# Weight and activation residues, state scaling and the norm's g moved from VectorE to GpSimd and ScalarE in a linear-attention and two-MoE kernel

## The chip, the cores and the metric

The kernel runs on one core of one Trainium2 chip. Its time is the device time in microseconds (us) of one launch; a median of several runs is given. Engines are named TensorE (PE in the profile, its weight loads PEld), VectorE (DVE), ScalarE (ACT), GpSimd (POOL) and SyncE (SP, which issues the DMAs).

## What is computed

Gated linear attention over 4 batches, 8 heads, 768 steps and a head size of 48, then two feed-forward blocks on the 3072 x 384 result. Weights arrive as 8-byte floats, all else as float32.

```python
for t in range(S):                      # attention, per batch and head
    state = alpha[t][:, None] * state + outer(k[t], v[t])
    y[t] = q[t] @ state
x = y as 3072 x 384
xn = x / sqrt(mean(x * x) + 1e-6) * rms_g        # first block, d_ff 1536
x = (silu(xn @ w_gate) * (xn @ w_val)) @ w_out
h = max(x @ w1, x @ w2, x @ w3)                  # second block, d_ff 768
out = h @ w_out2
```

## The kernel before

The attention is cut into 24 tiles of 128 steps (one batch, all heads; batches inside, steps outside). For each tile, class `Tile_` holds a chain: the loads of alpha, k, q (`ld`) and v (`lv`); for the first six tiles transposes on TensorE (`pa`), for the others on VectorE (`bt`); scans and products on VectorE that give R, kT (`br`) and aT, qT (`b`), with the old state scaled into Sd; transposed k and the scores on TensorE (`pb`); the scores masked on VectorE (`c`, tiles named at); state update and y on TensorE (`pc`); the sum of squares on ScalarE (`ss`), its root on GpSimd (`rr`, L702 and L705); the state's copy or sum (`st`); the normed, g-scaled row xn (`d`, L719); its transpose (`pd`); and the split of that into a rounded part xh (`eh`, ScalarE) and the residue xl (`el`, VectorE, L736).

Matmuls of the feed-forward blocks run on such pairs, a high part and a residue, in three products: high by high, residue by high, high by residue. The weights pass through class `Weights` in chunks of 128 x 384, two at a time: `load` (SP), `join` (VectorE, three instructions a chunk, L58 to L60, that make float32 out of the 8-byte words), `high` (ScalarE), `rest` (VectorE, the residue, L380) and `check` (ScalarE, two instructions on the raw words, L389 and L392, whose sums are looked at once at the end, by `flag`). There are 36 chunks of the first block, three for each of 12 columns blocks f (gate, val, out), and 24 of the second.

The first block runs in 96 slots, 12 for each of 8 blocks of 384 rows (three tiles); the slots of the first two blocks alternate in halves, so that slots 0 to 5 need the first 18 chunks and slots 12 to 17 the others. A slot has three groups of nine products on TensorE: gate, val (both at L769) and second (L816), with silu, a product on VectorE (`mu`, L802), and the split of the hidden row into hh (ScalarE) and hl (VectorE, L810) between them. The second block's 48 slots have four such groups.

The order of all this on each engine comes from a planner, class `Order`: each part has an engine, a cost, a due time (in slots) and the parts it needs; the planner plays this through and writes the instructions in the order found. Engines then run their own lists in that order and wait on semaphores. While TensorE has nothing to do before the first val product, the planner puts in filler products that nobody reads (`fill`, L776). The lines that set due times here:

```python
HEAD = (11, 2, 0, 1)
at = due(i) - (HEAD[i // 2] if first and i < 8 else 1 if first else 1.5)
if n < TPB:
    at, step = -20 + 2 * n, 0.5
elif n < 2 * TPB:
    at, step = -10 + 0.5 * (n - TPB), 1
```

Of the kernel before, what the change touches and what calls it, by code (L numbers as in the profile page):

```python
# [281 lines left out]
def gla_moe_moe(ctx: ExitStack, tc: tile.TileContext, q, k, v, alpha, wg, wv, wo, g, w1, w2, w3, wo2, out):  # L282
# [37 lines left out]
    HEAD = (11, 2, 0, 1)  # L320

    class Weights:


        def __init__(self, tag, pool, bufs, chunks, where, due, needs):

            self.tag, self.pool, self.raws, self.tmps = tag, pool, {}, {}
# [3 lines left out]
            for i in range(n):  # L331
                at = due(i) - 10 - (HEAD[i // 2] if first and i < 8 else 1.5)
                before = needs(i) + self.prev("load", i, 1) + self.prev("check", i, bufs)
                if i >= bufs:
                    before.append((tag, "join", (i - bufs) // 2 * 2))
                plan.add((tag, "load", i), "SP", 1.1, at, before, partial(self.load, i, bufs), later=LAT)
            for i in range(0, n, 2):
                both = [j for j in (i, i + 1) if j < n]
                at = due(i) - (HEAD[i // 2] if first and i < 8 else 1 if first else 1.5)
                plan.add((tag, "join", i), "DVE", 1.3 * len(both), at,  # L340
                         [(tag, "load", j) for j in both] + self.prev("rest", i, 2) + self.prev("join", i, 2),
                         partial(self.join, both))
                plan.add((tag, "high", i), "ACT", 0.45 * len(both), at, [(tag, "join", i)] + self.needed(needs, both),
                         partial(self.high, both))
# [9 lines left out]
        def needed(self, needs, both):  # L354
            return []

# [6 lines left out]
        def join(self, both):  # L363
            steps = []
            for i in both:
                self.tmps[i] = self.pool().tile([P, CW], F32, name="cv_t", bufs=2)
# [64 lines left out]
    gb = ap1.tile([P, DM], F32, name="gb")  # L431
# [8 lines left out]
    ends = ap1.tile([W, NP, P], F32, name="ends")  # L440
# [8 lines left out]
    column = ap1.tile([P, P], F32, name="column")  # L449
    place = ap1.tile([P, 32], F32, name="place")  # L450
# [31 lines left out]

    NPE = 6

    class Tile_:


        def __init__(self, n):
# [4 lines left out]

            if n < TPB:
                at, step = -20 + 2 * n, 0.5
            elif n < 2 * TPB:
                at, step = -10 + 0.5 * (n - TPB), 1
            elif n < 3 * TPB:
                at, step = 12 + 3 * (n - 2 * TPB), 1
            else:  # L500
                at, step = 21 + 4 * (n - 3 * TPB), 0.7
# [557 lines left out]
```

## Time and profile before

| | us |
|---|---|
| median of 3 runs | 906.6 (905.54 to 907.75) |
| the profiled execution | 905.86 |
| its span | 903.7 |
| TensorE busy in it | 886.8 |
| VectorE busy | 530.5 |
| ScalarE busy | 350.4 |
| GpSimd busy | 22.5 |

The span is what the profile covers of the profiled execution. Busy time of TensorE counts matmuls from start to modelled end, so overlaps and fillers count as busy. Idle time is shown ahead of the instruction that ended it, with what released it. The granted clock is 1.00 at TensorE's full 2.4 GHz. Instructions of one engine overlap a little: 0.55 us long, a VectorE residue is followed by the next after 0.47.

### The profile page before, as it was taken

What the parts mean: (1) busy time and instruction counts of PE and PEld (TensorE: products, weight loads), DVE (VectorE), ACT (ScalarE), POOL (GpSimd) and SP (SyncE); (2) the same over time, 40 slices, a digit from 0 to 9 for tenths busy, and PEclk for the clock granted to TensorE, in tenths of its full rate; (3) what the DMA queues carried; (4) which work ended last, traced back from release to release, by engine and by line L of the source; (5) the groups of instructions that cost most, each with busy time, mean ns of one, the idle gap of its engine ahead of it and who ended that gap; (6) DMA issues with size and microseconds to landing.
All of it is one profiled execution on the core that took longest, in us unless ns stands there. A gap on an engine that the chain in (4) does not pass through costs nothing.

```text
span 903.7 us, 16408 instructions
## 1 busy us (share of the span) xinstructions
PE 886.8 (98%) x6527; PEld 864.9 (96%) x6527; DVE 530.5 (59%) x1063; ACT 350.4 (39%) x898; POOL 22.5 (2%) x66
## 2 busy tenths in 40 slices
PE   7999999999999999999999999999999999999997
PEld 6889999999999999999999999999999999999996
DVE  8999999987666666666663377483332323323221
ACT  4578775333333223233233277561221212212121
POOL 1000000000000000000000000000000000000000
PEclk9999999999999999999999999999999999999999
DMA  9845654343223223223201145140110100101000
GB/s 196 190 114 159 193 168 131 101 123 84 58 57 85 57 58 84 58 58 81 61 10 45 36 131 164 39 140 17 37 53 1 53 27 27 53 1 53 1 27 30
DMA packets 106243, 69.17 MB, mean 77 GB/s; under 512 B 49200, under 2 KB 103856, under 8 KB 106160
## 3 DMA queue, kind: packets, MB, share of 16 engines
q1 hardware_dynamic: 106160, 68.05, 28.2%
q8 instruction: 53, 0.87, 0.4%
q14 instruction: 30, 0.25, 0.1%
HBM read 57.41 MB, written 10.62 MB: 75 GB/s over the span
## 4 chain that ended last, share of the span: by engine, by line
PE 89%; DVE 4%; DMA 3%; SPq 2%; ACT 1%; issue 1%; DVEq 0%; ACTq 0%
PE bank L769 56%; PE bank L816 15%; PE bank L969 8%; PE bank L653 2%; PE bank L691 2%; PE bank L685 2%; DMA raw<-in_moe_w_val_dram 1%; PE bank L676 1%; DVE cv_t L59 1%; DVE cv_t L60 1%; SPq L551 1%; PE bank L776 1%; PE bank L725 1%; SPq L562 1%; PE bank L646 1%
## 5 line engine op out<-in xcount | busy, mean ns | idle before, releaser
L954 DVE TENSOR_TENSOR sg<-sg,bank 128x384 f32<-128x384 f32 x96 | 53.2, 554 | 173.0 <-PE bank L769 172.7
L802 DVE TENSOR_TENSOR sg<-sg,bank 128x384 f32<-128x384 f32 x96 | 52.8, 550 | 94.5 <-PE bank L769 93.1
L806 ACT ACTIVATE hh<-sg 128x384 fp32r<-128x384 f32 x96 | 50.0, 520 | 134.4 <-DVE sg L802 134.3
L769 PE MATMUL bank<-xh,wgh 128*128 128x384 f32 x288 | 100.7, 350 | 0.0
L816 PE MATMUL bank<-hh,woh 128*128 128x384 f32 x288 | 98.3, 341 | 0.0
L769 PE MATMUL bank<-xl,wgh 128*128 128x384 f32 x288 | 97.2, 337 | 1.2 <-DVE xl L736 1.2
L816 PE MATMUL bank<-hl,woh 128*128 128x384 f32 x288 | 96.9, 336 | 1.3 <-DVE hl L810 1.3
L769 PE MATMUL bank<-xh,wgl 128*128 128x384 f32 x288 | 97.3, 338 | 0.1
L769 PE MATMUL bank<-xh,wvh 128*128 128x384 f32 x288 | 97.0, 337 | 0.0
L769 PE MATMUL bank<-xh,wvl 128*128 128x384 f32 x288 | 96.5, 335 | 0.0
L816 PE MATMUL bank<-hh,wol 128*128 128x384 f32 x288 | 96.4, 335 | 0.0
L769 PE MATMUL bank<-xl,wvh 128*128 128x384 f32 x288 | 96.3, 334 | 0.0
L958 ACT ACTIVATE hh<-sg 128x384 fp32r<-128x384 f32 x48 | 25.2, 525 | 160.0 <-DVE sg L954 160.0
L810 DVE TENSOR_TENSOR hl<-sg,hh 128x384 fp32r<-128x384 f32 x96 | 53.3, 555 | 31.3 <-ACT hh L806 31.3
L799 ACT ACTIVATE sg<-bank 128x384 f32<-128x384 f32 x96 | 46.7, 487 | 52.3 <-PE bank L769 51.3
L816 PEld LDWEIGHTS bank<-hl,woh 128*128 128x128 f32 x288 | 54.3, 188 | 2.4 <-DVE hl L810 2.3
L816 PEld LDWEIGHTS bank<-hh,woh 128*128 128x128 f32 x288 | 54.2, 188 | 1.8
L769 PEld LDWEIGHTS bank<-xl,wgh 128*128 128x128 f32 x288 | 54.5, 189 | 1.5 <-DVE xl L736 1.5
L769 PEld LDWEIGHTS bank<-xh,wgh 128*128 128x128 f32 x288 | 54.4, 189 | 1.5
L769 PEld LDWEIGHTS bank<-xh,wgl 128*128 128x128 f32 x288 | 54.5, 189 | 0.5 <-DVE wgl L380 0.5
L769 PEld LDWEIGHTS bank<-xh,wvh 128*128 128x128 f32 x288 | 54.1, 188 | 0.5 <-DVE sg L802 0.3
L816 PEld LDWEIGHTS bank<-hh,wol 128*128 128x128 f32 x288 | 54.2, 188 | 0.0
(138 smaller groups left out, 2010.9 us busy)
## 6 DMA issues: line engine op xcount, KB each, us to landing
raw<-in_moe_w_out_dram SPq DMA_DIRECT2D x18, 384.0 KB, 3.7
raw<-in_moe_w_dram SPq DMA_DIRECT2D x18, 384.0 KB, 3.8
y_scr<-yo SPq DMA_DIRECT2D x30, 192.0 KB, 2.0
raw<-in_moe_w_gate_dram SPq DMA_DIRECT2D x12, 384.0 KB, 4.3
vt<-in_v_dram SPq DMA_DIRECT2D x24, 192.0 KB, 2.7
raw<-in_moe_w_val_dram SPq DMA_DIRECT2D x12, 384.0 KB, 4.4
xl<-y_scr SPq DMA_DIRECT2D x8, 576.0 KB, 4.5
out_dram<-yo SPq DMA_DIRECT2D x24, 192.0 KB, 2.0
```

The costliest lines, as they stand in the source:

```text
L653: nc.tensor.matmul(self.sc[i][:, pr, :], self.kT[lo:hi, pr, :], self.qT[lo:hi, pr, :], start=True, stop=True)
L685: nc.tensor.matmul(self.y[tk, 2 * pr:2 * pr + 2, :].rearrange("p a d -> p (a d)"), self.qT[:, pr, tk], Sds[self.s][:, pr, :], start=True, ...
L691: nc.tensor.matmul(self.y[tk, 2 * pr + i, :], at[i][:, pr, tk], vt[:, 2 * pr + i, :], start=not self.c, stop=True, skip_group_check=True,)
L769: nc.tensor.matmul(ps, w_[:, kt, col], m_[:, kt, :], start=i == 0, stop=i == 3 * KT - 1)
L799: nc.scalar.activation(hid[s], banks[3][:, :NB], AF.Silu)
L802: nc.vector.tensor_tensor(hid[s], hid[s], banks[4][:, :NB], ALU.mult)
L806: nc.scalar.activation(hi_[s], hid[s], AF.Copy)
L810: nc.vector.tensor_tensor(lo_[s], hid.pop(s), hi_[s].bitcast(F32), ALU.subtract)
L816: nc.tensor.matmul(banks[e][:, :NB], w_[:, f, es], m_, start=f == f0 and i == 0, stop=f == f1 - 1 and i == 2)
L954: nc.vector.tensor_tensor(hid2[z], hid2[z], banks[3 + j][:, :NB], ALU.max)
L958: nc.scalar.activation(hi2[z], hid2[z], AF.Copy)
L969: nc.tensor.matmul(banks[t][:, :DM], l_[:, tsl], r_[:, f, :], start=f == 0 and i == 0, stop=f == NF2 - 1 and i == 2)
```

## The change

- The residues of the weights (`rest`), of both blocks, and of xt (`el`) go from VectorE to GpSimd. As GpSimd reads no PSUM here, ScalarE makes a second copy xf of the transposed row for it.
- The scaling of the old state into Sd goes to GpSimd, as a part of its own (`sd`, `carry`).
- g is no longer multiplied into xn: xn is made on ScalarE from y and the root alone, and GpSimd multiplies g into the gate and val chunks between `join` and `high` (`gain`; the tile gt holds g by columns).
- The first tiles' state copies (four tiles) go from VectorE to ScalarE; the square sums of kT are taken before those of qT.
- The first block's weights are checked later: each chunk is loaded a second time, from slot 27 on, and checked then. The buffer of a raw chunk is free for the next load after `join`, not after `check`; the joined chunks have four buffers instead of two.
- Due times of the first 12 tiles, of the transposes and of the chunks are new tables; the planner's cost of a group of products is 1.565 instead of 1.47.
- Some tiles share memory: column and place lie in aT, ends is BF16, xn has two buffers.

```diff
-    HEAD = (11, 2, 0, 1)
+    CV = 2
+    RAW = 4
+    AGAIN = 27
+    AHEAD = (
+        18.8, -3.3, 6.7, 4.1, 3, -3.1, 15.8, 2.3, -0.6, -0.8, 7.2, 23.8, 1.3, 1, 1, 1, 1, 1,
+    )
...
-                before = needs(i) + self.prev("load", i, 1) + self.prev("check", i, bufs)
+                before = needs(i) + self.prev("load", i, 1) + ([] if again else self.prev("check", i, bufs))
...
+                scaled = [j for j in both if self.scaled(j)]
+                if scaled:
+                    plan.add((tag, "gain", i), "POOL", 1.15 * len(scaled), at + 2.1, [(tag, "join", i), "gt"],
+                             partial(self.gain, scaled))
...
-                plan.add((tag, "rest", i), "DVE", 0.47 * len(both), at + 0.2, [(tag, "high", i)],
+                plan.add((tag, "rest", i), "POOL", 1.15 * len(both), at + (-4 if first else 0.2), [(tag, "high", i)],
                          partial(self.low, both))
                 for j in both:
-                    plan.add((tag, "check", j), "ACT", 1.42, at + 2, [(tag, "load", j)],
-                             partial(self.check, j))
+                    if again:
+                        old = [(tag, "check", j - bufs)] if j >= bufs else [(tag, "join", n - 2)]
+                        plan.add((tag, "load again", j), "SP", 1.1, again(j) - 2,
+                                 old + [(tag, "load again", j - 1) if j else (tag, "load", n - 1)],
+                                 partial(self.load, j, bufs), later=LAT)
+                    plan.add((tag, "check", j), "ACT", 1.42, again(j) if again else at + 2,
+                             [(tag, "load again" if again else "load", j)], partial(self.check, j))
...
+        def scaled(self, i):
+            return self.tag == "w1" and i % 3 < 2
+
+        def gain(self, which):
+            for i in which:
+                t = self.tmps[i].rearrange("p (a b) -> p a b", a=KT)
+                nc.gpsimd.tensor_tensor(t, t, gt.unsqueeze(2).to_broadcast([P, KT, P]), ALU.mult)
...
-                nc.vector.tensor_tensor(
+                nc.gpsimd.tensor_tensor(
                     dl, self.tmps.pop(i).rearrange("p (a b) -> p a b", a=a), dh.bitcast(F32), ALU.subtract
                 )
...
+        def carry(self):
+            for i, lo, hi in HALVES:
+                nc.gpsimd.tensor_tensor(
+                    Sds[self.s][lo:hi, :, i * D:(i + 1) * D], St[self.b][lo:hi],
+                    self.all[lo:hi].to_broadcast([D, NP, D]), ALU.mult,
+                )
...
-                    nc.vector.tensor_copy(St[self.b][lo:hi], self.U[lo:hi])
+                    nc.scalar.activation(St[self.b][lo:hi], self.U[lo:hi], AF.Copy)
...
-            nc.vector.scalar_tensor_tensor(self.xn, self.y, self.r[:, 1:2], gb, ALU.mult, ALU.mult)
+            nc.scalar.activation(self.xn, self.y, AF.Copy, scale=self.r[:, 1:2])
...
+            self.xf = ap.tile([P, KT, P], F32, name="xf", bufs=1)
+            nc.scalar.activation(self.xf, self.xt, AF.Copy)
...
-            nc.vector.tensor_tensor(
-                xl[self.blk][:, :, sl], self.xt, xh[self.blk][:, :, sl].bitcast(F32), ALU.subtract
+            nc.gpsimd.tensor_tensor(
+                xl[self.blk][:, :, sl], self.xf, xh[self.blk][:, :, sl].bitcast(F32), ALU.subtract
             )
...
-    MM = 1.47
+    MM = 1.565
```

How the order moves, at three places. GpSimd, from its first instruction that waits for another engine; before (r is the norm's root; the same two rows follow for each tile, up to the end):

```order
L702 TENSOR_SCALAR r<-stats 128x1
L705 TENSOR_TENSOR r<-r,half 128x1
```

and now, from the second pair of chunks to the third tile's xl (cv_t is a joined chunk, gt the g, wgl and wol weights' residues, xl that of the row):

```order
L383 TENSOR_TENSOR cv_t<-cv_t,gt 128x384
L408 TENSOR_TENSOR wol<-cv_t,woh 128x384
L408 TENSOR_TENSOR wgl<-cv_t,wgh 128x3x128
L776 TENSOR_TENSOR xl<-xf,xh 128x3x128
L738 TENSOR_SCALAR r<-stats 128x1
L741 TENSOR_TENSOR r<-r,half 128x1
L776 TENSOR_TENSOR xl<-xf,xh 128x3x128
L738 TENSOR_SCALAR r<-stats 128x1
L741 TENSOR_TENSOR r<-r,half 128x1
L383 TENSOR_TENSOR cv_t<-cv_t,gt 128x384 x3
L776 TENSOR_TENSOR xl<-xf,xh 128x3x128
L408 TENSOR_TENSOR wvl<-cv_t,wvh 128x3x128
```

What was an engine with two short instructions a tile now has the scalings and residues in one queue with them, and the third tile's xl stands behind three scalings more.

VectorE at the second tile (S is the first state, xn the normed row of the first tile); before:

```order
L714 COPY S_125<-bank_75 48x192 x2
L617 RECIPROCAL starts<-least 112x4
L620 SCALAR_TENSOR_TENSOR aT<-bank_80,starts 112x512
L630 TENSOR_TENSOR qT<-bank_74,aT 112x512
L719 SCALAR_TENSOR_TENSOR xn<-bank_76,r,gb 128x384
L380 TENSOR_TENSOR wgl<-cv_t,wgh 128x3x128
L380 TENSOR_TENSOR wvl<-cv_t,wvh 128x3x128
L604 COPY all<-bank_78 112x4
L605 MEMSET bank_78 112x4
```

and now:

```order
L650 RECIPROCAL starts<-least 112x4
L653 SCALAR_TENSOR_TENSOR aT<-bank_80,starts 112x512
L657 TENSOR_TENSOR qT<-bank_74,aT 112x512
L58 TENSOR_SCALAR cv_t<-raw 128x384 x2
L59 SCALAR_TENSOR_TENSOR cv_t<-raw,cv_t 128x384 x2
L60 SCALAR_TENSOR_TENSOR cv_t<-raw,cv_t 128x384 x2
L702 TENSOR_TENSOR at<-bank_79,mask 128x512
L702 TENSOR_TENSOR at<-bank_80,mask 128x512
L637 COPY all<-bank_73 112x4
```

The copy of S, xn and the two residues are gone from between the second tile's products, and the second pair of chunks has moved up into their place.

TensorE shortly before the first gate, at the fifth tile's transposes (in_al, in_kk, in_qq) and the third tile's xn; before:

```order
L579 MATMUL bank_74<-ident,in_al 112x128 x4
L579 MATMUL bank_75<-ident,in_kk 112x128 x4
L579 MATMUL bank_78<-ident,in_qq 112x128 x4
L725 MATMUL bank_79<-ident,xn 128x128 x3
L776 LDWEIGHTS ident
L776 MATMUL bank_77<-mask,ident 128x256
```

and now (line numbers are those of the changed kernel):

```order
L612 MATMUL bank_79<-ident,in_al 112x128 x4
L612 MATMUL bank_80<-ident,in_kk 112x128 x4
L612 MATMUL bank_73<-ident,in_qq 112x128 x4
L761 MATMUL bank_76<-ident,xn 128x128 x3
L815 LDWEIGHTS ident
L815 MATMUL bank_77<-mask,ident 128x256
```

Before, 30 of the pairs of the last two rows, the fillers, follow there, then the fourth tile's scores, then the first gate. Now nine such pairs follow, then the fourth tile's state and y, nine fillers, then the first gate. In all there are 191 fillers before and 143 now; all other matmuls are the same in number.

## Rows read from the trace of the kernel before

**Rows 1.** The page, busy time of each engine, share of the span, instructions.
```profile
PE 886.8 (98%) x6527; PEld 864.9 (96%) x6527; DVE 530.5 (59%) x1063; ACT 350.4 (39%) x898; POOL 22.5 (2%) x66
```

**Rows 2.** Windows; length, busy time of PE, PEld, DVE, ACT, POOL, clock, DMA share, GB/s.
```profile
49.25:93.00 43.75, 41.35 (x392) 38.51 (x391) 42.15 (x97) 34.24 (x96) 2.77 (x6) 0.96 0.49 143
93.00:150.00 57.00, 56.81 (x397) 55.60 (x398) 55.21 (x117) 42.53 (x119) 0.92 (x2) 1.00 0.61 176
...
300.00:400.00 100.00, 100.00 (x877) 97.15 (x876) 64.53 (x121) 31.01 (x79) 3.69 (x10) 1.00 0.25 61
...
500.00:600.00 100.00, 99.80 (x621) 98.76 (x620) 58.75 (x127) 57.82 (x153) 0.74 (x2) 1.00 0.33 102
```

**Rows 3.** Timeline of PE; start, length, line, instruction, count, idle time before it.
```profile
16.85 0.57 PE L676 MATMUL bank<-vt,kn 128*48 128x48 f32 x16 [1.16 <-ACT kn L659]
...
37.02 5.09 PE L776 MATMUL bank<-mask,ident 128*128 128x256 bf16 x45
...
49.25 0.44 PE L769 MATMUL bank<-xh,wgh 128*128 128x384 f32 x1
...
52.99 1.10 PE L691 MATMUL bank<-vt,at 128*64 128x48 f32 x32
...
598.16 0.44 PE L816 MATMUL bank<-hl,woh 128*128 128x384 f32 x1 [0.20 <-DVE hl L810]
```

**Rows 4.** Window after two waits of PE, same columns as rows 2.
```profile
66.00:72.00 6.00, 5.90 (x35) 5.15 (x34) 5.51 (x13) 4.57 (x15) 0.00 (x0) 0.72 0.65 204
```

**Rows 5.** Timeline of DVE up to the first gate.
```profile
5.38 0.16 DVE L604 COPY all<-bank 112x4 f32<-112x4 f32 x1 [0.41 <-PE bank L579]
...
9.86 0.35 DVE L58 TENSOR_SCALAR cv_t<-raw 128x384 int32<-128x384 int32 x1
...
29.02 0.63 DVE L58 TENSOR_SCALAR cv_t<-raw 128x384 int32<-128x384 int32 x2
...
31.56 0.62 DVE L719 SCALAR_TENSOR_TENSOR xn<-bank,r,gb 128x384 f32<-128x384 f32 x1
32.10 1.28 DVE L666 TENSOR_TENSOR at<-bank,mask 128x512 f32<-128x512 f32 x2
33.29 0.55 DVE L380 TENSOR_TENSOR wol<-cv_t,woh 128x384 fp32r<-128x384 f32 x1
33.76 0.55 DVE L380 TENSOR_TENSOR wgl<-cv_t,wgh 128x384 fp32r<-128x384 f32 x1
...
46.67 0.18 DVE L617 RECIPROCAL starts<-least 112x4 f32<-112x4 f32 x1 [1.14 <-ACT junk L480]
...
48.03 0.69 DVE L626 TENSOR_TENSOR Sd<-S,all 48x192 f32<-48x192 f32 x2
```

**Rows 6.** Groups of POOL's memsets; busy us, mean ns, idle before.
```profile
L444 POOL MEMSET starts<- 112x512 f32 x1 | 0.6, 603 | 0.0
...
L437 POOL MEMSET in_al<- 128x256 f32 x1 | 0.3, 311 | 0.0
```

**Rows 7.** Groups of DVE, the two of line 456.
```profile
L456 DVE TENSOR_SCALAR ident<-column,place 32x128 f32<-32x128 f32 x4 | 2.0, 499 | 0.1
...
L456 DVE TENSOR_SCALAR mask<-column,place 32x128 f32<-32x128 f32 x4 | 1.1, 279 | 0.1
```

**Rows 8.** Timeline of POOL, and of DVE (the last row) beside it.
```profile
54.87 0.19 POOL L702 TENSOR_SCALAR r<-stats 128x1 f32<-128x1 f32 x1 [16.20 <-ACT junk L480]
55.15 0.55 POOL L705 TENSOR_TENSOR r<-r,half 128x1 f32<-128x1 f32 x1
74.87 0.75 POOL L702 TENSOR_SCALAR r<-stats 128x1 f32<-128x1 f32 x1 [19.18 <-ACT junk L480]
...
74.55 1.02 DVE L60 SCALAR_TENSOR_TENSOR cv_t<-raw,cv_t 128x384 int32<-128x384 int32 x2
```

**Rows 9.** Groups of ACT, the two instructions of a check.
```profile
L392 ACT ACTIVATE junk<-junk,bound 128x384 bf16<-128x384 bf16 x60 | 37.0, 616 | 2.0
L389 ACT ACTIVATE junk<-raw 128x384 bf16<-128x384 f32 x60 | 32.9, 548 | 20.5 <-DMA raw<-in_moe_w_val_dram 11.5 <-DMA raw<-in_moe_w_out_dram 4.9 <-DMA raw<-in_moe_w_gate_dram 3.2
```

More of the change, by code (lines that the diff above doesn't have):

```diff
@@ L319, in gla_moe_moe, with __init__ @@
     LAT = 2.2
-    HEAD = (11, 2, 0, 1)
+    CV = 2
[4 more added lines that the diff above has]
+    )
     class Weights:
-        def __init__(self, tag, pool, bufs, chunks, where, due, needs):
+        def __init__(self, tag, pool, bufs, cv, chunks, where, due, needs, again=None):
+            self.cv = cv
             self.tag, self.pool, self.raws, self.tmps = tag, pool, {}, {}
@@ L331, in __init__ @@
             for i in range(n):
-                at = due(i) - 10 - (HEAD[i // 2] if first and i < 8 else 1.5)
-                before = needs(i) + self.prev("load", i, 1) + self.prev("check", i, bufs)
+                at = due(i) - 10 - (AHEAD[i // 2] + 2.4 if first else 1.5)
+                before = needs(i) + self.prev("load", i, 1) + ([] if again else self.prev("check", i, bufs))
                 if i >= bufs:
@@ L430, in gla_moe_moe @@
     half = ap1.tile([P, 1], F32, name="half")
-    gb = ap1.tile([P, DM], F32, name="gb")
+    gt = ap1.tile([P, KT], F32, name="gt")
     ins, halves = [], []
@@ L439, in gla_moe_moe @@
     R = ap1.tile([W, NP, P], F32, name="R")
-    ends = ap1.tile([W, NP, P], F32, name="ends")
+    ends = ap1.tile([W, NP, P], BF16, name="ends")
     starts = ap1.tile([W, NP, P], F32, name="starts")
@@ L447, in gla_moe_moe @@
     St = [ap1.tile([W, NP, D], F32, name=f"S{b}") for b in range(B)]
-    column = ap1.tile([P, P], F32, name="column")
-    place = ap1.tile([P, 32], F32, name="place")
+    column, place = aT[:, 0, :], aT[:, 1, 0:32]
     nc.vector.memset(mask, 1.0)
@@ L492, in __init__ @@
             c, last = self.c, self.c == NC - 1
[L494 to L501, printed above, removed]
+            at, step = DUES[n] if n < len(DUES) else (21 + 4 * (n - 9), 0.7)
             def t(kind, m=n):
@@ L508, in add @@
                 needs = needs + [last_one if last_one in plan.parts else None]
-                plan.add(t(kind), engine, cost, at + step * i, needs, run, **kw)
+                plan.add(t(kind), engine, cost, at + step * i + (SHIFT.get(kind, 0) if n < 9 else 0), needs, run, **kw)
             r = room(n)
@@ L534, in __init__ @@
             add("pc", "PE", (1.4 if c else 0.9) + (0 if last else 0.5), 2.5,
-                [t("c"), t("lv"), None if last else t("kn")], self.pe_c, banks=1 if last else 2,
+                [t("c"), t("lv"), None if last else t("kn"), t("sd") if c else None], self.pe_c, banks=1 if last else 2,
                 until=[t("d")] + ([] if last else [t("st")]), room=r)
@@ L743, in give @@
             held.remove(i)
-    plan.add("gb", "SP", 0.6, -21, [("t", "ld", 0)],
-             lambda: nc.sync.dma_start(out=gb, in_=g.unsqueeze(0).to_broadcast([P, DM])), later=2.0)
+    plan.add("gt", "SP", 0.6, -21, [("t", "ld", 0)],
+             lambda: nc.sync.dma_start(out=gt, in_=g.rearrange("(k p) -> p k", p=P)), later=2.0)
     for n in range(NT):
```

61 lines of the change are left out of this document (35 added, 26 removed).

## The prediction, made before the changed kernel was run

> **What bounds the kernel now.** I read the page's head first, then the windows, then TensorE's own timeline, then VectorE's and GpSimd's instructions. The head shows TensorE busy for 886.8 of 903.7 us and VectorE for 59% [rows 1]. The windows tell where this average hides something: later TensorE is busy without a break (100 us of 300 to 400, 99.8 of 500 to 600), while from the first products to 150 us VectorE too is busy for 96 to 97% of the time [rows 2]. So only the first 150 us or so can give anything, and two things are to be had there.
>
> First, the time until the first gate product. It starts at 49.25 us, and until then TensorE runs the short matmuls of the first tiles and 191 filler products that compute nothing [rows 3]. The 45 fillers of one row take 5.09 us, 0.113 each with the last one's tail, 0.110 without: 21 us for all 191. Second, small waits. Leaving out the wait for the first input, TensorE is idle nine times, first at 16.85 and last at 598 us, 6.0 us in all, seven of the nine behind VectorE [rows 3]. After two of these, at 64 and 65 us, the granted clock is 0.72 on average over 66 to 72 us, part of it at the lower of the two levels (1.2 instead of 2.4 GHz) [rows 4]; 0.28 x 6 = 1.7 us are lost. From the first gate on, then, TensorE does real work or waits for VectorE, and VectorE has no air: the two tie. A change that only unloads VectorE gains the waits; to gain more it has to bring the first gate forward.
>
> **The change part by part.** *TensorE's fillers.* The new order has 143 of them, 48 fewer, and the same matmuls of real work in all: 48 x 0.110 = **-5.3 us**, if nothing idle comes in their place. TensorE's own rows up to the gate would end at 49.25 - 5.3 - 2.4 (the three waits ahead of it) + 1.5 (a fourth tile's last products, now ahead of the gate: the L691 at 52.99 us and the eight ahead of it) = 43 us [rows 3]. Are the gate's inputs there by then? Ahead of them VectorE has, in the new order, the scans and products of four tiles (4.4 us each: from 5.38 to 9.86 us in the first), four pairs of chunks joined (2.5 us) and three maskings (1.2 us): 17.6 + 10.2 + 3.6 = 31.4 us after 5.4, so 36.8 us [rows 5]. Before, it also had there half a fifth tile, three pairs of S copies, three xn, four residues of weights and three of xl, for one pair of chunks less. Behind VectorE GpSimd then has two scalings and the residue of the third tile, some 3 us by the price below: 40 us. That leaves 3 us of lead, and the fillers really go.
>
> *TensorE's waits.* The 6.0 us and the 1.7 us of clock go if VectorE keeps ahead: **-7.7 us**. Ahead of the residue hl of slot 10, the eleventh, VectorE loses 24 residues of weights and 6 of xl (0.47 us from start to start), 6 xn (0.54), 6 scalings Sd (0.36) and 8 copies of S (0.37) [rows 5]: 11.3 + 2.8 + 3.2 + 2.2 + 3.0 = 22.5 us. The new order spends 16 of these on work it draws forward (two more tiles' scans and products, a masking pair, two more chunks, three more transposes). VectorE is thus 6.5 us earlier there by its own work and 2.3 by waits for ScalarE and GpSimd that go (the longest 1.14 us [rows 5]). TensorE is 1.5 us earlier by its own (the fillers less a seventh tile's products) and 6.6 by waits and clock. Before they tied to about half a microsecond, so VectorE now leads by about 1 us at slot 10. By slot 16 both orders have joined all chunks, and there VectorE keeps about 22 us. So what VectorE loses up to slot 10, beyond 1 us, is paid by TensorE; later losses are not.
>
> *GpSimd's price.* No row shows it on 128x384 with two inputs. From below: its memsets write 256 columns in 0.31 and 512 in 0.60 us without reading any, so 384 in 0.46 [rows 6]. From above: their slope, 0.29/256 = 1.14 ns a column, three times over for two reads and a write, is 1.3 us, with 0.2 for the start 1.5. I take 1.0, the middle, as neither row is nearer. The Trainium skill (GPSIMD Engine Reference, Engine selection) has GpSimd about twice as slow as VectorE on two-input work, by VectorE's 0.55 us an estimate of 1.1, and by that the sum would be 1 us longer. Up to slot 10 GpSimd gets 26 residues of weights, 18 scalings and 6 residues of xl (50 at 1.0), 8 halves of Sd at half the width (4 us) and nine norms of 0.83 us (7) [rows 8]: 61 of 105 us. It fits.
>
> *The two engines in each other's way.* Here the trace speaks against the change. The same VectorE instruction on 32x128 (L456) takes 0.499 us on average while GpSimd's memsets run and 0.279 after them [rows 7]. GpSimd's one-column L702, 0.19 us else, takes 0.75 at 74.87 us and ends just behind two L60 of VectorE, which read two SBUF tensors each [rows 8]. Each holds up the other. Ahead of slot 10 VectorE's instructions of these kinds (L58 to L60 of 28 chunks, 11 hl, scans and products of three tiles out of SBUF) take 33.9 + 5.2 + 11.0 = 50 of 105 us. Bounds of what this costs VectorE: nothing, if GpSimd always is the one to wait, as L702 did; 50 x 1.0 x 50/105 = 24 us, if each of GpSimd's instructions stops VectorE for its whole length. In between: these instructions form 31 runs on VectorE, and at three of the four ahead of the gate GpSimd has nothing to do; it is busy at the start of 61/105 = 0.58 of the other 28, with half an instruction left: 28 x 0.58 x 0.5 = 8 us. The L456 row gives much the same, 0.22 us for each memset of 0.5, or 44% of those 24, 10.5. I take 8, less the lead of 1: **+7 us**.
>
> *The rest at nothing.* ScalarE gains xn, a second copy of xt and the first S copies, each some 0.5 us, but loses 36 checks of 1.2 us and more [rows 9] from its fullest stretch (34 of 44 us busy [rows 2]). The checks come back from slot 27 on, 42 us and more over some 200, where it is 31% busy; between 500 and 600 us it was 58% busy with such checks, and TensorE 99.8% [rows 2]. Without that cover a check would hold up a silu by its own length, and TensorE has two products (3.1 us) to do before it needs that bank. The 36 new loads of 384 KB use queues that move 61 GB/s there and moved 176 between 93 and 150 us [rows 2]; a load that waits for a check holds the tile loads behind it on SP, but those are due 15 slots before their block. In the second set of weights 24 residues go to GpSimd, and a pair of chunks takes 1 us longer; TensorE at 99.8% covers it, and it would wait that 1 us otherwise. The load of g in 4-byte pieces takes the place of another one; GpSimd's first scaling waits for it, and a microsecond there is inside the gate's lead.
>
> The sum: -5.3 - 7.7 + 7 = -6.0 us. The profiled execution took 905.86 us, 0.7 below the median of 906.6; from the median that makes **900.6 us**.
>
> **The rivals.** *GpSimd alone waits.* It fits itself in behind VectorE's runs, as L702 did, and VectorE loses nothing: all 13 us come, 893.6. For it the 0.75 of L702, against it L456. Chance 0.2.
>
> *GpSimd stops VectorE (slower).* Each of its instructions holds VectorE for its full length where both want SBUF, up to slot 10: 24 - 1 = 23 us of waits at TensorE, and at least one more fall of the clock, 1.7 us: 906.6 - 13 + 23 + 1.7 = 918.3. Its sign turns where VectorE loses 14 us, 0.28 us for each of the 50 instructions. For it L456, which was held in all its four; against it that L456 stood against a row of memsets without a gap, and that no row shows VectorE behind a GpSimd instruction that reads. The Trainium skill (SBUF — State Buffer, Who interferes with whom) states the lock outright: a VectorE instruction with two SBUF inputs and a GpSimd one that reads SBUF exclude each other for the whole instruction. By that rule this rival is the case; L702 agrees for GpSimd's side, VectorE's side no run here has shown yet. Chance 0.2.
>
> *GpSimd becomes the bound.* At 1.5 us an instruction it has 86 of 105 us, and some 12 us of its own waits behind VectorE besides; weights come late at slots 3 to 10, waits take the fillers' place, and of the 13 us about none is left: 906. Only the upper price speaks for it. Chance 0.1.
>
> **How the numbers follow.** The forecast has 0.5 (896 to 905 by itself), the rivals 0.2, 0.2 and 0.1. A measurement of this kernel can tell about 0.2%, 1.8 us, from no change. Faster: GpSimd alone waiting, and nearly all of the forecast, 0.67. Same: GpSimd as the bound and the forecast's tail, 0.13. Slower: 0.2. The range runs from just below the best case, 892.5, half way into the slower one, 912.
>
> **What would show it.** Right: the first gate near 43 us, no filler after it; TensorE's waits up to 150 us under 8 us; L59 and L60 stretched from 0.55 to some 0.7 us on average before slot 10; GpSimd's residues near 1.0 us. Wrong: the first gate above 46 us; TensorE behind residues on GpSimd (GpSimd the bound); L59 and L60 at 0.55 throughout (GpSimd alone waits) or at 1 and more (VectorE stopped); more falls of the granted clock.

## The result and the profile after

The change makes the kernel slower: 910.62 us (907.74 to 916.92, 18 runs) against 905.93 (904.59 to 907.75) for the kernel before, ratio 1.0054, 95% interval 1.004 to 1.0068. Forecast were 900.6 and "faster". The profiled execution of the changed kernel took 913.86 us, 3.2 over its own median; the sums below are made for it. Its mean granted clock, 0.990, is the lowest but one of the 18 runs (0.989 to 0.996), so the share of the clock is larger in these sums than in most runs.

First the page's busy times and the windows, as [rows 1] and [rows 2]; the third window is new, and its row of before stands behind the others. Columns of the windows: stretch, length, busy PE, PEld, DVE, ACT, POOL, granted clock, DMA share, GB/s.

```profile
PE 887.3 (97%) x6479; PEld 864.4 (95%) x6479; DVE 489.4 (54%) x907; ACT 372.9 (41%) x954; POOL 183.3 (20%) x214
```

```profile
49.25:93.00 43.75, 39.67 (x353) 37.09 (x353) 41.37 (x76) 19.68 (x52) 34.07 (x32) 0.96 0.54 150
93.00:150.00 57.00, 51.90 (x341) 50.43 (x342) 51.47 (x91) 23.74 (x57) 35.27 (x30) 0.94 0.57 166
200.00:220.00 20.00, 18.22 (x139) 16.99 (x139) 13.75 (x25) 12.46 (x37) 5.41 (x6) 0.91 0.66 185
300.00:400.00 100.00, 100.00 (x838) 97.18 (x836) 55.45 (x100) 35.60 (x90) 16.08 (x23) 1.00 0.24 59
500.00:600.00 100.00, 100.00 (x625) 99.01 (x624) 48.64 (x98) 55.57 (x147) 20.20 (x20) 1.00 0.27 84
```
```profile
200.00:220.00 20.00, 20.00 (x179) 19.37 (x179) 15.50 (x31) 6.46 (x17) 0.74 (x2) 1.00 0.33 88
```

VectorE has 41 us less to do, and nothing changes after 300 us. But from the gate to 150 us, where TensorE stood idle for a few us before, it is now busy for 91% of the time, at 0.94 to 0.96 of its clock (0.96 and 1.00 before). TensorE's timeline (start, length, instruction, idle time before it and what ended it), as [rows 3]:

```profile
45.10 0.42 PE L808 MATMUL bank<-xh,wgh 128*128 128x384 f32 x1
...
70.64 1.70 PE L689 MATMUL bank<-qT,kT 48*128 48x128 f32 x16 [1.89 <-ACT xn L755]
...
96.12 0.69 PE L808 MATMUL bank<-xh,wvh 128*128 128x384 f32 x1 [4.31 <-DVE sg L841]
...
136.55 0.44 PE L808 MATMUL bank<-xh,wvh 128*128 128x384 f32 x1 [1.08 <-DVE sg L841]
...
210.67 0.44 PE L808 MATMUL bank<-xh,wvh 128*128 128x384 f32 x1 [1.61 <-DVE sg L841]
```

The gate starts 4.15 us sooner. All waits but the first input's make 13.8 us (15 of them), 6.0 before. The granted clock costs 0.04 x 43.75 + 0.06 x 57 + 0.09 x 20 = 7.0 us in the first three windows, 0.04 x 43.75 = 1.75 before [rows 2]. So: 48 fillers -5.3, waits +7.8, clock +5.3: +7.8 us, of the 8.0 between the two profiled executions.

Why VectorE is late is seen where the longest wait arises: its own timeline, and GpSimd's beside it.

```profile
39.74 0.36 DVE L58 TENSOR_SCALAR cv_t<-raw 128x384 int32<-128x384 int32 x1 [1.98 <-DMA raw<-in_moe_w_val_dram]
...
87.48 2.66 DVE L59 SCALAR_TENSOR_TENSOR cv_t<-raw,cv_t 128x384 int32<-128x384 int32 x2
90.06 1.64 DVE L60 SCALAR_TENSOR_TENSOR cv_t<-raw,cv_t 128x384 int32<-128x384 int32 x2
91.62 1.27 DVE L702 TENSOR_TENSOR at<-bank,mask 128x512 f32<-128x512 f32 x2
92.82 1.06 DVE L618 STREAM_TRANSPOSE aT<-in_al 128x512 f32<-128x512 f32 x1
...
95.55 0.53 DVE L841 TENSOR_TENSOR sg<-sg,bank 128x384 f32<-128x384 f32 x1
```

```profile
87.31 1.12 POOL L408 TENSOR_TENSOR wvl<-cv_t,wvh 128x384 fp32r<-128x384 f32 x1
88.40 1.33 POOL L408 TENSOR_TENSOR wol<-cv_t,woh 128x384 fp32r<-128x384 f32 x1
89.68 1.60 POOL L663 TENSOR_TENSOR Sd<-S,all 48x192 f32<-48x192 f32 x2
```

A pair of L59 takes 2.66 us instead of 1.02 while GpSimd works on residues. Behind it in VectorE's list stand a masking and three transposes drawn forward, and only then the product with sg (L841) that TensorE is waiting for. VectorE's groups from 16 to 100 us (busy us, mean ns), after and then before, show which instructions stretch:

```profile
L59 DVE SCALAR_TENSOR_TENSOR cv_t<-raw,cv_t 128x384 int32<-128x384 int32 x18 | 12.3, 724 | 0.0
L60 DVE SCALAR_TENSOR_TENSOR cv_t<-raw,cv_t 128x384 int32<-128x384 int32 x18 | 9.8, 584 | 0.0
L58 DVE TENSOR_SCALAR cv_t<-raw 128x384 int32<-128x384 int32 x20 | 8.0, 428 | 3.5 <-DMA raw<-in_moe_w_val_dram 2.5 <-DMA raw<-in_moe_w_gate_dram 1.0
L702 DVE TENSOR_TENSOR at<-bank,mask 128x512 f32<-128x512 f32 x12 | 7.7, 683 | 0.0
...
L849 DVE TENSOR_TENSOR hl<-sg,hh 128x384 fp32r<-128x384 f32 x6 | 4.5, 747 | 1.4 <-ACT hh L845 1.4
...
L645 DVE TENSOR_SCALAR least<-R 112x4 f32<-112x4 f32 x7 | 3.0, 433 | 0.2
```

```profile
L59 DVE SCALAR_TENSOR_TENSOR cv_t<-raw,cv_t 128x384 int32<-128x384 int32 x20 | 10.2, 552 | 0.0
L60 DVE SCALAR_TENSOR_TENSOR cv_t<-raw,cv_t 128x384 int32<-128x384 int32 x20 | 10.2, 551 | 0.0
L666 DVE TENSOR_TENSOR at<-bank,mask 128x512 f32<-128x512 f32 x10 | 6.4, 682 | 0.0
L58 DVE TENSOR_SCALAR cv_t<-raw 128x384 int32<-128x384 int32 x20 | 6.2, 354 | 0.0
...
L612 DVE TENSOR_SCALAR least<-R 112x4 f32<-112x4 f32 x5 | 0.8, 170 | 0.2
```

The stretched ones read SBUF alone; those that read PSUM (L702, before L666) keep their length. With 18 x 0.172 (L59), 18 x 0.033, 20 x 0.074, 7 x 0.263 (L645), 6 x 0.196 (hl, 0.551 before) and 0.5 of L652 (VectorE's small product in `all`) that is 8.7 us in these 84.

It also goes the other way. A residue of GpSimd that starts 0.2 us after a run of VectorE's joins takes 3.62 us instead of 1.0, and the joins keep their length. The root r stands behind it in GpSimd's queue, ScalarE's xn waits for r, and TensorE then waits 1.89 us for xn at 70.64. GpSimd, VectorE, ScalarE:

```profile
62.29 3.62 POOL L408 TENSOR_TENSOR wvl<-cv_t,wvh 128x384 fp32r<-128x384 f32 x1 [0.64 <-ACT wvh L402]
```
```profile
62.61 1.02 DVE L59 SCALAR_TENSOR_TENSOR cv_t<-raw,cv_t 128x384 int32<-128x384 int32 x2
```
```profile
70.01 0.58 ACT L755 ACTIVATE xn<-bank,r 128x384 f32<-128x384 f32 x1 [0.77 <-POOL r L741]
```

### The profile page after: what moved, and what is told of

Same layout as the page of the kernel before. It is cut to its first block, busy times and chain, and to the rows that moved or that the text cites. A ratio compares the mean times of both kernels' runs of the same rounds, so it can differ in the third digit from the quotient of the medians.

```text
span 912.1 us, 16466 instructions
## 1 busy us (share of the span) xinstructions
PE 887.3 (97%) x6479; PEld 864.4 (95%) x6479; DVE 489.4 (54%) x907; ACT 372.9 (41%) x954; POOL 183.3 (20%) x214
## 4 chain that ended last, share of the span: by engine, by line
PE 81%; DVE 8%; DMA 4%; issue 2%; ACT 2%; POOL 1%; SPq 1%; DVEq 0%; ACTq 0%; POOLq 0%
PE bank L808 52%; PE bank L855 14%; PE bank L1008 8%; DMA raw<-in_moe_w_val_dram 2%; PE bank L689 2%; PE bank L727 1%; PE bank L721 1%; DVE cv_t L59 1%; DMA raw<-in_moe_w_gate_dram 1%; PE bank L815 1%; DVE cv_t L60 1%; DVE cv_t L58 1%; DMA in_kk<-in_k_dram 1%; DVE sg L841 1%; DVE at L702 1%
## 5 line engine op out<-in xcount | busy, mean ns | idle before, releaser
L841 DVE TENSOR_TENSOR sg<-sg,bank 128x384 f32<-128x384 f32 x96 | 53.0, 552 | 120.7 <-PE bank L808 116.7
L849 DVE TENSOR_TENSOR hl<-sg,hh 128x384 fp32r<-128x384 f32 x96 | 59.8, 622 | 62.0 <-ACT hh L845 61.9
L776 POOL TENSOR_TENSOR xl<-xf,xh 128x384 fp32r<-128x384 f32 x24 | 36.3, 1514 | 93.3 <-ACT xf L771 87.4
L808 PEld LDWEIGHTS bank<-xh,wvl 128*128 128x128 f32 x288 | 54.9, 190 | 0.0
```

The lines of the kernel that those rows point to most:

```text
L776: nc.gpsimd.tensor_tensor(xl[self.blk][:, :, sl], self.xf, xh[self.blk][:, :, sl].bitcast(F32), ALU.subtract)
L808: nc.tensor.matmul(ps, w_[:, kt, col], m_[:, kt, :], start=i == 0, stop=i == 3 * KT - 1)
L841: nc.vector.tensor_tensor(hid[s], hid[s], banks[4][:, :NB], ALU.mult)
L849: nc.vector.tensor_tensor(lo_[s], hid.pop(s), hi_[s].bitcast(F32), ALU.subtract)
```

## The experiments

The theory after this reading: GpSimd stops VectorE. The rival: the order made anew for the change is at fault, whatever engine does the residues. "Old order" below means the order of the kernel before; each median stands beside a kernel before of 905.5 to 905.9.

### What a GpSimd instruction takes from VectorE

**Pairs alone.** A row of trials behind the last product:

```diff
+    both(none, 0, rest, 6)
+    both(none, 0, gain, 6)
+    for vs in (one_in, two_in, two_f32, one_bank, turned):
+        both(vs, 6, none, 0)
+        both(vs, 12, rest, 6)
+        both(vs, 12, fill, 8)
+    both(two_in, 12, gain, 6)
```

> The changed kernel with a row of trials put behind its last product: forms of VectorE's instructions alone, then twelve of them beside six GpSimd residues (two SBUF inputs, 128x384) or eight GpSimd memsets, both engines released together. Its time is longer by the trials and means nothing else. Theory (GpSimd's reading instructions and VectorE's two-input ones shut each other out): 12 two-input instructions (0.47 us alone) beside 6 residues (1.0 us alone) take nearly the sum, 5.6 + 6.0 = 11 to 12 us together, and single VectorE instructions of about 1.5 us stand among those of 0.55; with one input out of PSUM, and for the 128x512 transposes, nothing changes, as the 0.68 and 1.08 us in the changed kernel's trace; one input: in between. Rival (GpSimd alone gives way): VectorE needs 5.6 us in every pair and GpSimd ends later. Rival (each slows the other a little, no exclusion): all 12 instructions are stretched alike, to 0.6 or 0.7 us, none above 1.

VectorE's timeline there: twelve instructions with one input beside six residues; with two beside residues, then beside memsets; with one input out of PSUM beside residues; with two beside six multiplications by g. Then GpSimd's: residues and multiplications alone, residues beside the two-input ones.

```profile
927.80 8.79 DVE L295 TENSOR_SCALAR v_c<-v_raw 128x384 int32<-128x384 int32 x12
...
947.43 11.15 DVE L298 SCALAR_TENSOR_TENSOR v_c<-v_raw,v_a 128x384 int32<-128x384 int32 x12
...
958.99 7.07 DVE L298 SCALAR_TENSOR_TENSOR v_c<-v_raw,v_a 128x384 int32<-128x384 int32 x12
...
994.30 8.66 DVE L304 TENSOR_TENSOR v_c<-bank,v_b 128x512 f32<-128x512 f32 x12
...
1038.50 10.14 DVE L298 SCALAR_TENSOR_TENSOR v_c<-v_raw,v_a 128x384 int32<-128x384 int32 x12
```

```profile
912.99 6.33 POOL L310 TENSOR_TENSOR g_c<-g_a,g_b 128x384 f32<-128x384 f32 x6 [8.31 <-issue]
...
919.42 5.34 POOL L314 TENSOR_TENSOR g_a<-g_a,g_g 128x384 f32<-128x384 f32 x6
...
947.27 7.33 POOL L310 TENSOR_TENSOR g_c<-g_a,g_b 128x384 f32<-128x384 f32 x6
```

Two-input work takes 7.07 us beside memsets, as alone (six in 3.51), and 11.15 beside residues: each residue takes 4.1 / 6 = 0.68 us from VectorE and itself grows from 1.05 to 1.22. While both run in these trials they take turns, one VectorE instruction every 1.23 to 1.26 us. One-input work is hit as hard (six alone in 2.33 us, so 4.1 of the 8.79 are lost): there the expectation of something in between was wrong. A multiplication by g takes 3.1 / 6 = 0.51. PSUM input and transposes lose nothing. So a residue saves VectorE 0.47 us and can cost it 0.68. The Trainium skill (SBUF — State Buffer, Who interferes with whom) states that two-input VectorE work and GpSimd's reads exclude each other for the whole instruction, and that GpSimd's pure writes do not disturb it. The trace agrees on both for two-input work, but a pair took 1.25 us, less than the 1.05 + 0.58 of a full exclusion.

**The weights' work taken off GpSimd.**

```diff
-                nc.gpsimd.tensor_tensor(dl, self.tmps.pop(i)..., dh.bitcast(F32), ALU.subtract)
+                nc.scalar.activation(dl, self.tmps.pop(i)..., AF.Copy)   # first set only
-                nc.gpsimd.tensor_tensor(t, t, gt.unsqueeze(2).to_broadcast([P, KT, P]), ALU.mult)
+                pass
```

> The changed kernel in its own order, with GpSimd's work on the first set of weights taken away: the multiplication by g is left out, and the low part of a weight is a ScalarE copy instead of a GpSimd difference (so g and the true low parts are missing from the result). Theory (the loss is VectorE's, stopped by GpSimd): VectorE's second join step falls from 0.72 back to 0.55 us up to 100 us, TensorE's waits up to 150 us from 12 to under 6 us, the granted clock there stays at 1, and 910.6 - 7 - 4 = about 900 us (897 to 904). Rival (the new order itself is too tight, with 48 fillers fewer and work drawn forward): the waits near 70 and 96 us stay and it takes 907 to 911.

902.91 us (898.87 to 905.04; ratio 0.9943 to 0.9975): 7.7 less than the changed kernel. L59 is back at 0.550 us, and the clock at 1.00 up to 150 us. The wait of 1.89 us behind xn is gone too. Yet TensorE still has 10.7 us of waits; the two longest:

```profile
72.33 0.56 PE L715 MATMUL bank<-vt,kn 128*48 128x48 f32 x16 [1.67 <-DVE at L705]
...
90.94 0.44 PE L811 MATMUL bank<-xh,wvh 128*128 128x384 f32 x1 [2.97 <-DVE sg L844]
```

Both accounts hold in part. GpSimd's weights are worth 7.7 us, against a kernel in which neither engine does this work; and the order keeps long waits without them, that for sg at the same place, the one at 72.33 for another instruction than the 1.89 us of before. The wait of 2.97 us cost no clock here.

**g through ScalarE, and residues on VectorE again**, two variants in the changed kernel's order:

```diff
+                nc.scalar.activation(self.xf[:, i, :], self.xt[:, i, :], AF.Copy, scale=gt[:, i:i + 1])
+            nc.scalar.activation(xh[blk][:, :, sl], self.xf, AF.Copy)
```
```diff
-                nc.gpsimd.tensor_tensor(   # the weights' low
+                nc.vector.tensor_tensor(
```

> The changed kernel in its own order, but g goes in on ScalarE, as the scale of three copies out of the transposed y (xf), and GpSimd's multiplications by g are gone; residues of weights stay on GpSimd, the result is the reference's. Theory (each GpSimd instruction takes time from VectorE, 0.52 us for a multiplication by g and 0.69 for a residue where VectorE is in joins): of the 7.7 us that both were worth, the 18 multiplications up to slot 10 hold 18 x 0.52 / (18 x 0.52 + 26 x 0.69) = a third, 2.6 us: 908 (906 to 909.5), L59 near 0.65 us. Rival (the residues alone do it, or ScalarE's longer chain gives it back): 910 to 912.

> The changed kernel in its own order, with all residues of weights back on VectorE; g, Sd, xl and the norm stay on GpSimd, the result is the reference's. Up to slot 10 VectorE gets 26 x 0.47 = 12 us more work, and loses less to GpSimd, which there keeps 32 of its 58 two-input instructions: theory (about 9 us lost now, in proportion to GpSimd's instructions): 4 to 5 us come back, so 910.6 + 12 - 5 = about 917 (913 to 921). Rival (GpSimd costs VectorE as much as it takes off it): 908 to 912. Rival (only the order was wrong): 922, the whole 12 us as waits.

With g on ScalarE 908.77 us (ratio 1.0011 to 1.0041): 1.9 of the expected 2.6 came. With the residues on VectorE 912.32 (1.0042 to 1.0082): its 12 us of extra work up to slot 10 cost only 1.7, and not clear of noise (the changed kernel's interval is 1.004 to 1.0068). That is close to the first rival: in this order a residue costs VectorE about as much on GpSimd as on itself.

### Engine or order

**The late checks alone**, once with an order made anew by the planner, once set into the old order:

```diff
+                    if again:
+                        plan.add((tag, "load again", j), "SP", 1.1, again(j) - 2, ..., later=LAT)
+                    plan.add((tag, "check", j), "ACT", 1.42, again(j) if again else at + 2, ...)
```
```diff
+        out = [n for n in out if n not in w1]          # w1: the checks, in the planned list
+        for n in w1:
+            for name, slot in ((("w1", "load again", n[2]), 25), (n, 27)):
+                out.insert(out.index(("mu", slot + n[2])) + 1, name)
```

> The kernel before with one part of the change alone: the checks of the first set of weights come later, on a second load of each chunk; GpSimd's and VectorE's shares are as before. Theory (the late checks are nearly free and only GpSimd costs): 21 fillers go, 2.3 us, nothing else moves: 903.6 (901.5 to 905.5), and no wait of over 1 us from 150 us on. Rival (the second loads and the checks that come back collide with the silu chain, as the 1.61 us wait at 210.67 us of the changed kernel could be): 907 to 910, with waits behind ScalarE or behind late tiles between 150 and 300 us.

> The kernel before with its own order on all engines and its 191 fillers; only the checks of the first set of weights are taken out and set down, each on a second load of its chunk, from slot 27 on. Late checks alone with an order made anew took 908.6. Theory A (the order made anew did that, with 21 fillers fewer and residues due later on VectorE; checks and loads by themselves cost nothing and free ScalarE): 904 to 906. Theory B (the second loads and the returned checks cost the 3 us): 907.5 to 910, with waits from 150 us on.

908.63 us with the new order (ratio 1.0024 to 1.0045), 903.16 with the old one (0.9964 to 0.9983). Engines and instructions are the same, but for 21 fillers that the slower one does not have: 5.5 us are order. TensorE's timeline and the clock of the new order, then the clock of the old one:

```profile
81.12 0.45 PE L774 MATMUL bank<-xh,wgl 128*128 128x384 f32 x1 [1.93 <-DVE wgl L385]
89.71 0.47 PE L774 MATMUL bank<-xh,wgl 128*128 128x384 f32 x1 [3.28 <-DVE wgl L385]
```
```profile
49.25:93.00 43.75, 36.70 (x355) 33.23 (x354) 43.17 (x97) 16.18 (x42) 3.23 (x6) 0.93 0.59 156
```
```profile
49.25:93.00 43.75, 41.08 (x398) 38.00 (x398) 42.89 (x97) 19.63 (x47) 3.72 (x6) 1.00 0.51 152
```

The expected rival's time came with another cause than it named: from 150 to 340 us TensorE has no wait over 0.1 us, so the second loads and the returned checks cost nothing. In the old order they are even worth 2.7 us.

**Residues on GpSimd in the old order.**

```diff
-                nc.vector.tensor_tensor(   # the weights' low, in the variant just above
+                nc.gpsimd.tensor_tensor(
```

> The variant with late checks in the old order (903.2, VectorE's residues of weights) with one thing changed: the residues of both sets of weights go to GpSimd, each at its old place in the order. With the same pair in the new order (910.6 with GpSimd, 912.3 with VectorE) this separates engine and order. Theory A (a residue on GpSimd takes from VectorE's joins, at 0.69 us each where they meet, about what it saves, 0.47; the new order is the larger loss): 902 to 906. Rival (GpSimd's share alone is a clear gain and the order alone lost): 897 to 901. Rival (GpSimd's share is itself the loss): 907 to 912.

904.21 us (0.9975 to 0.9992), 1.05 more than with VectorE, with overlapping intervals. One row of VectorE and one of GpSimd show what a residue can do, and a window where the clock falls:

```profile
60.76 0.97 DVE L620 TENSOR_SCALAR least<-R 112x4 f32<-112x4 f32 x1
```
```profile
60.68 1.03 POOL L388 TENSOR_TENSOR wgl<-cv_t,wgh 128x384 fp32r<-128x384 f32 x1
```
```profile
49.25:93.00 43.75, 40.53 (x389) 38.05 (x389) 38.65 (x80) 18.71 (x44) 16.42 (x20) 0.96 0.51 149
```

An instruction over four columns, 0.17 us else, waits out a whole residue; TensorE's wait for the scan behind it grows from 0.84 to 1.97 us. Other waits shrink, so that all together are 4.9 us, with VectorE 5.0; the clock of 49.25 to 93 us is 0.96 instead of 1.00. So GpSimd instead of VectorE for the residues is worth +1.1 us in the old order and -1.7 in the new one, which also carries the other parts of the change: next to nothing, and in neither order clear of noise. The new order costs 5.5 us with the same engines (the late checks), and 6.4 and 9.2 between the pairs with the residues on GpSimd and on VectorE, where the other parts of the change are in it. From 905.9 us, then, the late checks take 2.7, the residues on GpSimd add 1.1 and all the rest 6.4. How these 6.4 divide is not shown: xl, Sd and the multiplication by g on GpSimd were never tried in the old order.

### Attempts on the new order

**Honest costs, three moves, fillers back**: a join counted 1.6 instead of 1.3 us; three pieces of VectorE's list behind what TensorE waits for, in the changed kernel and in the variant with g on ScalarE; 48 more fillers.

```diff
-                plan.add((tag, "join", i), "DVE", 1.3 * len(both), at,
+                plan.add((tag, "join", i), "DVE", 1.6 * len(both), at,
```
```diff
+        for late, first in ((("t", "bt", 6), ("t", "c", 5)), (("t", "bt", 7), ("mu", 5)), (("t", "b", 11), ("mu", 24))):
+            out.remove(late)
+            out.insert(out.index(first) + 1, late)
```
```diff
+            for _ in range(48 if name == ("g", 0) else 0):
+                self.fill()
```

> The changed kernel with one number of the planner altered: a chunk's join counts 1.6 us instead of 1.3 (measured up to 100 us: 0.43 + 0.72 + 0.58 = 1.74; 1.46 before), so that VectorE's order is made for what the joins take beside GpSimd. It has 169 fillers instead of 143, 2.9 us. Theory A (the waits of 1 to 4 us behind VectorE, and the falls of the clock after them, come from an order that is late by the stretch): waits up to 150 us fall from 12 to about 6 us and the clock stays at 1, 910.6 + 2.9 - 6 - 4 = 903.5 (902 to 907). Theory B (VectorE's work is too much there in any order): 909 to 913.

> The changed kernel with three pieces of VectorE's queue put one place back, nothing else: the transposes (L618) of tile 6 behind the masking that TensorE waits for, those of tile 7 behind the product with sg of slot 5, the second scan of tile 11 behind the product with sg of slot 24. Theory A (in VectorE's queue work that is not yet needed stands ahead of work that TensorE waits for, and each such wait also costs a fall of the clock): the wait of 4.31 us at 96.12 falls to about 1.5, the one of 1.61 at 210.67 to 0.6, the clock in 93 to 150 and 200 to 220 us comes back to 1 (4 us): 910.6 - 2.8 - 1 - 3 = 904 (902 to 907). Theory B (VectorE has too much to do there whatever stands first): the moved pieces are late next, waits only change places, 909 to 911.5.

> The variant with g as the scale of ScalarE's copies (908.8) with the same three pieces put back. Theory A: its waits of 4.45 us at 95.27 and 1.87 at 75.26 go down to 1.5 and 0, the granted clock of 93 to 120 us comes back from 0.87 to 1 (3.5 us): 908.8 - 3 - 1.9 - 3 = 901 (899 to 904), under the kernel before. Theory B: 907 to 910.

> The changed kernel with 48 filler products more, right ahead of the first gate product, 191 as in the kernel before: 5.3 us that TensorE spends on nothing. Theory (up to 150 us VectorE sets the pace, and a gate that comes earlier only waits later): the waits after the gate shrink by as much and the clock falls less, 908 to 912. Rival (TensorE's own row sets the time, the waits are there in any case): 915 to 917.

Honest join costs: 919.90 us (ratio 1.0146 to 1.0180), worse than both theories; one number of the planner moves the time by 9 us (2.9 of them 26 more fillers), with a new wait of 3.67 us at 59.56. Three moves: 911.13 (1.0038 to 1.0065), theory B. The wait of 4.31 became 1.88 and that of 1.61 went, but 1.64 at 82.39, 0.94 at 98.92, 1.79 at 114.08 and 3.12 us at 263.37 came. With g on ScalarE 907.04 (1.0007 to 1.0033), at the edge of B. Fillers back: 916.91 (1.0111 to 1.0145), the rival: each of the 48 costs 0.13 us, no less than its own 0.11. One row of VectorE shows a reason:

```profile
53.42 0.55 DVE L843 TENSOR_TENSOR sg<-sg,bank 128x384 f32<-128x384 f32 x1 [3.10 <-PE bank L810]
```

VectorE's list has the first product with sg ahead of the next joins, so a later gate holds VectorE up as well, and it can't use the time. So VectorE is not simply the bound: here each of the two engines waits for the other.

### Parts without GpSimd, and fewer fillers

The ScalarE moves (xn, first S copies, g as the scale of its copies, late checks) with an order made anew, and in the old order; the latter with every fifth filler out; the late checks in the old order with fewer fillers, with the S copies alone on ScalarE, and with both.

```diff
-            nc.vector.scalar_tensor_tensor(self.xn, self.y, self.r[:, 1:2], gb, ALU.mult, ALU.mult)
+            nc.scalar.activation(self.xn, self.y, AF.Copy, scale=self.r[:, 1:2])
-                    nc.vector.tensor_copy(St[self.b][lo:hi], self.U[lo:hi])
+                    nc.scalar.activation(St[self.b][lo:hi], self.U[lo:hi], AF.Copy)
```
```diff
+        fills = [i for i, n in enumerate(out) if n is None]
+        out = [n for i, n in enumerate(out) if i not in fills[4::5]]
```

> The kernel before with the parts of the change that lay nothing on GpSimd: the late checks, the normed y and the first S copies on ScalarE; g comes in as the scale of ScalarE's copies and in VectorE's xl out of PSUM. Residues, Sd and xl stay on VectorE; the result is the reference's. It has 88 fillers, 103 fewer than before (11.3 us). Theory (VectorE is the bound and only relief without GpSimd counts): VectorE loses 6 x 0.4 + 8 x 0.37 = 5.4 us up to slot 10 against the late checks alone (908.6), and the clock falls go: 908.6 - 5.4 - 2 = 901 (899 to 904), faster than both kernels. Rival (the earlier gate is paid back by waits again, or ScalarE becomes the bound with the checks moved behind): 906 to 911.

> Late checks in the old order, and besides the normed y and the first S copies on ScalarE, g as the scale of ScalarE's copies and in VectorE's xl out of PSUM: the parts of the change that lay nothing on GpSimd, with the order of the kernel before. With an order made anew the same parts took 908.2. Theory A (VectorE's 5.4 us less up to slot 10 take away its four waits of 3.2 us in all): 900 (899 to 902). Rival (the longer ScalarE chain from y to xh puts new waits in their place): 903 to 907.

> The variant before in this list with every fifth filler left out, 153 instead of 191, nothing else. Theory A (the fillers ahead of the gate are TensorE's own time, as 48 added ones cost 6.3 us, and the gate's inputs are there 4 us sooner with VectorE relieved): 4.2 us less, 896 (894 to 898). Rival (the gate's inputs come no sooner; a wait takes the fillers' place): the same time as with 191, within 1 us, or 1 to 3 us more where the clock falls.

> Late checks in the old order (903.2), with every fifth filler left out, 153 instead of 191. Theory A (a filler is worth its 0.11 us where the gate's inputs are there): up to 38 x 0.11 = 4.2 us, 899 to 901.5. Theory B (VectorE's work ahead of the gate and behind it ties; the waits behind its scans near 46 and 63 us grow by what the fillers give, as 1.7 us came of 4.2 in the variant with ScalarE moves): 901.5 to 903.5.

> Late checks in the old order (903.2) with the first S copies on ScalarE alone, nothing else moved: VectorE has eight copies of 0.37 us less up to the gate and just behind it, and no chain gets longer but S's own. Theory A (VectorE's relief takes from the waits near 63 us, 0.84 and 0.31, and lets the gate start 0.5 sooner): 902.2 (901.5 to 903). Theory B (the gate that comes sooner only makes the wait behind VectorE's scan longer, with a fall of the clock, as the ScalarE moves did: 905.2): 904 to 906.

> Both: late checks in the old order, first S copies on ScalarE, 153 fillers. Theory A: the two gains add, 898 to 901. Theory B: VectorE's work behind the gate keeps the time, 901.5 to 904.

| variant | median, us | ratio, 95% |
|---|---|---|
| ScalarE moves, new order, 88 fillers | 908.22 | 1.0016 to 1.0038 |
| ScalarE moves, old order | 905.23 | 0.9989 to 1.0006 |
| the same, 153 fillers | 903.50 | 0.9966 to 0.9984 |
| late checks, old order | 903.16 | 0.9964 to 0.9983 |
| the same, 153 fillers | 903.91 | 0.9966 to 0.9985 |
| late checks, S copies on ScalarE | 903.56 | 0.9972 to 0.9990 |
| the same, 153 fillers | 902.48 | 0.9950 to 0.9977 |

Theory A missed throughout; the rival or Theory B held in three of the six (908.22, 905.23 and 902.48), while 903.50, 903.91 and 903.56 lie outside both. Relief of VectorE ahead of the gate buys nothing by itself: the ScalarE moves in the old order are 2.1 us slower than the late checks alone. And 38 fewer fillers (4.2 us) bring 1.7 us at most. Why is in the trace of the late checks with 153, TensorE's timeline and one window:

```profile
46.65 0.44 PE L779 MATMUL bank<-xh,wgh 128*128 128x384 f32 x1
...
105.64 0.44 PE L826 MATMUL bank<-hl,woh 128*128 128x384 f32 x1 [1.80 <-DVE hl L820]
```
```profile
93.00:150.00 57.00, 55.20 (x381) 53.97 (x380) 52.23 (x113) 24.05 (x57) 0.99 (x2) 0.97 0.57 168
```

The gate starts 1.46 us sooner (48.11 with 191): the rest went into waits ahead of it. Behind it a wait of 1.80 us is new, and a fall of the clock takes 0.03 x 57 = 1.7. The last variant has the lowest median found, 3.2 us under the kernel before; its interval lies below 1, but overlaps with those of four other variants here.

## Why the prediction was wrong

- **Fillers, -5.3 us:** the 48 went, none ran behind the gate. The gate came at 45.1 us instead of 43: VectorE stood idle for 1.98 + 0.37 us at 39.74 and 37.40 for chunks of weights that had not arrived. The working had VectorE never waiting for a load.
- **TensorE's waits, -7.7 us "if VectorE keeps ahead":** this step failed. With the +7 of the two engines, waits and clock were to come out 0.7 us shorter; in the profiled execution they came out 13.1 longer. The variant without GpSimd's weights took 904.43 us in its own profiled execution, 9.4 less, so that much of the 13.1 is GpSimd's. What is left, +3.7 (+2.7 by the medians: 902.9 against 905.5, with 5.3 us of fillers fewer), stands where -7.7 was forecast, though VectorE has neither the residues nor GpSimd's weights beside it there. The step made a balance of VectorE's work at one point, slot 10, and found a lead of 1 us. But the lists run in order: a lead counts only if the next instruction in the list is the one that is wanted. The late checks alone lost 5.5 us to a new order with VectorE's and GpSimd's shares as before. What makes the old order good was not found; three moves and a truer cost did not give it.
- **The clock:** priced at one fall of 1.7 us that would go; it cost 7.0 in the profiled execution. Without GpSimd's weights it cost some 1.7 (0.06 of the 20 us from 200, 0.01 of the 50 before). So of the 9.4 us between these two executions about 5.3 were clock and 3.2 waits (13.8 against 10.7).
- **Two engines in each other's way, +7:** near in size (8.7 us of stretch up to 100 us; 7.7 in the median time), but in part by luck: the forecast had it all as waits of TensorE, and more of it was lost clock. L59 went to 0.72 us as foretold, L60 only to 0.58. VectorE's side, which no row of before had shown, is now shown.
- **GpSimd's price, 1.0 us:** 1.05 for a residue alone, 0.89 for a multiplication by g. Right, and in the changed kernel TensorE waits nowhere directly for GpSimd.
- **The rest at nothing:** right for loads and checks, which are even a gain of 2.7 us in the old order. Left out was ScalarE's xn as a link: it waits for r, and r now stands in GpSimd's queue behind work on weights (1.89 us of TensorE at 70.64). The ScalarE moves, too, cost 2.1 us in the old order.
- **The rivals:** "GpSimd stops VectorE" had one of the mechanisms and the sign, and set its turn at 14 us of VectorE's loss. The sign turned although VectorE lost only 8.7, because the gains that were to pay for it were not there. "GpSimd alone waits" happened as well, at 62.29 us, but not throughout. The range (892.5 to 912) held the time.

## What to carry to other kernels

Where engines run fixed lists in order, change engine and order apart: put the one part into the old list first. Here that showed a gain of 2.7 us that a new plan turned into a loss of 3.1. Before moving SBUF work from VectorE to GpSimd, set what it saves (0.47 us here) against what it takes from VectorE's SBUF instructions meanwhile (0.68); beside VectorE's instructions with a PSUM input, or its transposes, the trials showed no loss. A wait of TensorE of over a microsecond is worth pricing with the fall of the clock that can follow it (0.94 from 93 to 150 us with the wait of 4.31, but 1.00 with that of 2.97).

## What was not expected

A VectorE instruction over four columns can be held for a whole GpSimd residue: 0.97 instead of 0.17 us. One-input tensor_scalar work (L58) loses as much to a GpSimd residue as two-input work, and a little to memsets too: twelve took 6.01 us beside eight memsets, some 4.7 alone. Forty-eight fillers added ahead of the gate cost 6.3 us, thirty-eight taken away in the old order gained 1.7 at most.
